# Larger score units and larger attention sums in a fused attention and two-layer kernel, under a new written order

## The chip, the cores and the metric

The kernel runs on one core of a Trainium2 chip. The metric is the device time of one execution in microseconds (us). Three runs of the kernel before gave 293.12, 293.34 and 293.79, median 293.34 us.

## The reference

Eight batches, eight heads, 576 positions, 64 values a head; q, k, v are fp32, drawn with a standard deviation of 0.1. Heads 0 to 3 see a window of 32 positions; heads 4 to 7 see every fourth position of the last 128. The rows of the attention, 4608 tokens x 512, go through two layers, 512 to 2048 and back to 512.

```python
scores = (q @ k.T) / 8
mask_plain = (rel >= 0) & (rel < 32)                     # heads 0-3
mask_dil = (rel >= 0) & (rel < 128) & (rel % 4 == 0)     # heads 4-7
attn = softmax(where(mask, scores, -1e9))
x = (attn @ v).transpose(0, 2, 1, 3).reshape(4608, 512)
h = x @ moe_w_in
out = (h * sigmoid(h)) @ moe_w_out                       # (4608, 512) fp32
```

## The kernel before

**The written order.** The whole kernel is a list of small steps, and TABLE (lines 11 to 121) is their order, written out by hand. Each word of it names a step, and every engine and every DMA queue works off its own instructions in that order. The first time a name stands there, a TensorE (PE) step issues its matmuls, and the letter behind "=" says in which PSUM bank (a, b, x, y, u, z; s is a pair of banks). Each later word of the same name issues the next instruction that follows: =A on ScalarE (ACT), =D on VectorE (DVE), =S a store on SP's queue, =P a sum on POOL; no letter, whatever engine the step has fixed. Steps without matmuls issue their first instruction at their first word. GpSimd (POOL) issues the casting loads and a few sums.

The names: the number in front is the batch, or, for l, y, u and t, the group of tokens. N0 to N3 cast raw q and k (0, 1 are k, 2, 3 are q), N4 to N11 clear the probability buffers; TD, TR, TA, TS transpose q and k on PE for batches 0 to 2 (PEB = 3); T are the transposing loads (SP's queue) that do this for batches 3 to 7; S is a score unit; V copies v, O shifts rows of v; P and D are attention sums of the plain and of the dilated heads; XP and XD transpose their outputs into xA, the input of layer 1; batches 5 to 7 write them to a scratch in DRAM (W, stores on SP) and read them transposed (X). L loads v for a batch and starts the cast of a later batch's q and k (its words: vraw, vp, cast); B does so for batch 2 and casts batch 3; M turns the additive mask into one of ones and zeros. l is layer 1, y layer 2, and u, w, v, a, t are the sums that the seven-product form of both layers needs (lines 885 to 943, 1004 to 1055). f are small POOL copies that hold loads back; z is a filler matmul (line 1082) into a bank nobody reads; exp and silu load an activation table ahead.

**Scores** (lines 601 to 647). A block is 128 keys by 96 queries (plain, "p", 12 a batch) or by 72 (dilated, "d", 16 a batch), for two heads (p) or two residues of a head (d) at once, each in a bank; the contraction is 64 long, so that a score matmul uses 64 of the 128 rows of PE's array. SETS says which blocks make a unit: batches 0 to 2 have seven units of four blocks, the others six (4, 4, 4, 6, 6, 4). A unit is one Exp, or one a bank, and one DVE multiply by its mask (line 647), read from mask_p or mask_d. Batch 0 (BIASED) has no multiply: the mask, as a large negative number, is put into the bank first by a matmul with the identity (line 616). Probabilities lie in 8 buffers (NP), taken in turn.

**Attention sums** (lines 685 to 712). The probabilities are the weights, v with a column of twos behind it the moving side: 65 columns, the last of which is the denominator. A block here is one head's 96 or 72 queries: 24 plain and 32 dilated a batch. A step takes four into one bank, then DVE does a reciprocal (line 691) and a multiply (line 693). A batch has 6 P steps (`av_p`) and 8 D steps (`av_d`). The dilated v goes from `vraws`, as loaded, to `vds` with its column of twos (line 671).

**Layers.** Groups of tokens are 256, 256, and then eight of 512. Group 0's layer 1 needs XP0 to XP2 and XD0 of batch 0. Groups 0 and 1 use plain layer 2 (line 954), the rest the seven-product form (line 1015); layer 1 uses line 830, and the seven-product form (line 918) for half of group 7 and for groups 8 and 9.

**The start.** Two loads on SP bring batch 0's raw k and q for the dilated heads; POOL issues the others. Lines 347 to 385 are memsets, the identity, the masks and the clears of the v buffers (lines 351 to 355, one ACT copy each); eight matmuls and the fillers keep PE running until data comes.

Of the kernel before, what the change touches and what calls it, by code (L numbers as in the profile page):

```python
# [19 lines left out]
l1.7=b 0B l1.2=s l1.7=t l1.7 l1.0=a l1.0=t l1.0 l1.15=y l1.15=s l0.13=u l0.14=x l1.3=y l0.14=s l1.3=t l0.15=a  # L20
l0.13=s l0.5=b l0.5=s l0.15=s 0B l0.9=u l1.3 0M l0.12=x l1.4=y 0N11=D l0.12=s l1.4=s l0.8=b l0.8=s l0.9=s
l1.6=z l1.1=x l1.1=s 1TD2=b l0.4=a l0.4=s 1TD2=D l1.6=s 1TD1=u 1TD1=D l1.10=y l1.10=s 1TA1k=a 1TA1k=A l1.12=z
1TD0=x l0.6=y l1.12=s l0.6=s 1TD0=D l1.11=a l1.11=s 1TD3=u 1TD3=D 1TA0k=y 1TA0k=D 1TA0q=x 1TA0q=D l1.9=z
1TS0=a 1TA1q=u 1S6=yb 1S6 1S6 l1.9=t 1TA1q=A 1V1=D 1O2 1TS1=x 1S3=s 1TS1=D y0.0.0=y 1TS1=D 1TS0=A 1TS0=A l1.9
1S3 l1.8=b w0 1S4=za 1S4 1S4 l1.8=t l1.8 l1.5=u 1S3 1S2=s 1S2 1S6 1S5=zx 1S5 y0.0.1 1S5 1S2 1S1=s l1.5=t l1.5
1S0=ba 1S0 1S3 y0.1.0=z l1.13=b 1S0 1V0=D l1.13=s 1D12=a y0.1.1 1D12 1S4 l1.14=x l1.14=s y0.1.2 1D01=u 1D12
# [100 lines left out]
def kernel(  # L127
# [12 lines left out]
    P = 128  # L140
# [983 lines left out]
```

## Time and profile before

| what | us |
|---|---|
| median of three runs (lowest, highest) | 293.34 (293.12, 293.79) |
| the profiled execution | 293.66 |
| its span, first instruction to last | 291.9 |
| its granted TensorE clock | 1.0 throughout |

The busy time of each engine by stage of that execution:

| stretch (us) | PE | DVE | ACT | POOL |
|---|---|---|---|---|
| 4.5 to 23.6 (batch 0 up to layer 1 alone) | 17.28 of 19.10 | 14.74 | 13.97 | 13.80 |
| 23.6 to 288.6 | 264.79 of 265.00 | 207.72 | 178.21 | 41.93 |
| 288.6 to 291.9 (last copies and stores) | 0.11 of 3.30 | 0.00 | 0.37 | 0.00 |

PE is the matmuls, PEld the weight loads, which overlap them. In the rows that follow L12 is line 12 of the kernel, "128x512 f16 x16" the shape of an operand and the number of instructions in a group; "[0.28 <-issue]" is idle time of the engine ahead of an instruction and what ended it.

### The profile page before, as it was taken

What the parts mean: (1) busy time and instruction counts of PE and PEld (TensorE: products, weight loads), DVE (VectorE), ACT (ScalarE), POOL (GpSimd) and SP (SyncE); (2) the same over time, 40 slices, a digit from 0 to 9 for tenths busy, and PEclk for the clock granted to TensorE, in tenths of its full rate; (3) what the DMA queues carried; (4) which work ended last, traced back from release to release, by engine and by line L of the source; (5) the groups of instructions that cost most, each with busy time, mean ns of one, the idle gap of its engine ahead of it and who ended that gap; (6) DMA issues with size and microseconds to landing.
All of it is one profiled execution on the core that took longest, in us unless ns stands there. A gap on an engine that the chain in (4) does not pass through costs nothing.

```text
span 291.9 us, 7564 instructions
## 1 busy us (share of the span) xinstructions
PE 285.5 (98%) x3006; PEld 205.1 (70%) x3006; DVE 225.3 (77%) x671; ACT 196.3 (67%) x411; POOL 58.8 (20%) x93
## 2 busy tenths in 40 slices
PE   7999999999999999999999999999999999999995
PEld 2568855655576777458567776588668888888884
DVE  5794477888985887666686869788999977949971
ACT  5787794598688477765966965548666656407931
POOL 8854724003720060034000071000000000000000
PEclk9999999999999999999999999999999999999999
DMA  8999999999999979989994749987620221112003
GB/s 158 183 202 197 192 195 186 201 186 187 128 206 202 209 126 199 184 160 82 216 200 78 196 74 192 237 190 186 182 61 24 78 57 74 54 56 110 3 2 142
DMA packets 98731, 42.30 MB, mean 145 GB/s; under 512 B 67208, under 2 KB 94344, under 8 KB 98696
## 3 DMA queue, kind: packets, MB, share of 16 engines
q0 software_dynamic: 46464, 19.21, 54.3%
q1 hardware_dynamic: 49784, 18.29, 29.2%
q10 hardware_dynamic: 2448, 4.33, 4.2%
q8 instruction: 23, 0.38, 0.5%
q14 instruction: 12, 0.10, 0.1%
HBM read 39.19 MB, written 17.10 MB: 193 GB/s over the span
## 4 chain that ended last, share of the span: by engine, by line
PE 90%; DMA 6%; POOL 2%; DVE 0%; issue 0%; ACT 0%; ACTq 0%
PE y L1015 33%; PE h L830 30%; PE h L918 11%; PE y L954 5%; DMA w_in<-in_moe_w_in_dram 4%; PE s L628 4%; PE av_d L688 3%; DMA nat<-in_q_dram 2%; PE av_p L688 2%; POOL w_in L388 1%; PE td L543 1%; PE xd L744 1%; PE xp L728 1%; POOL vp L333 1%; PE ta_k L577 0%; PE ta L590 0%
## 5 line engine op out<-in xcount | busy, mean ns | idle before, releaser
L830 PE MATMUL h<-xA,w_in 128*128 128x512 f16 (+1 forms) x480 | 101.5, 351 | 0.1
L839 ACT ACTIVATE gT<-h 128x512 f16<-128x512 f32 (+1 forms) x102 | 53.3, 543 | 29.2 <-PE h L830 28.1
L830 PEld LDWEIGHTS <-w_in 128*128 128x128 f16 x480 | 43.1, 97 | 30.7 <-DVE oD L693 0.5
L1015 PEld LDWEIGHTS <-gT 128*128 128x128 f16 x512 | 48.2, 98 | 6.9
L1015 PE MATMUL y<-w_out,gT 128*128 128x256 f16 x384 | 48.3, 273 | 0.0
L1015 PEld LDWEIGHTS <-work 128*128 128x128 f16 x384 | 36.7, 98 | 6.1 <-issue 0.3
L1015 PE MATMUL y<-w_sum,work 128*128 128x256 f16 x256 | 32.0, 273 | 0.1
L1042 DVE TENSOR_TENSOR ob<-y,nat 128x256 f32<-128x256 f32 x48 | 20.1, 421 | 14.2 <-PE y L1015 11.7
L688 PEld LDWEIGHTS <-probs 128*128 128x128 f16 x448 | 23.0, 97 | 10.6 <-ACT probs L637 0.6
L693 DVE TENSOR_TENSOR oD<-av_d,rcps 72x256 f16<-72x256 f32 x64 | 25.9, 414 | 1.1
L637 ACT ACTIVATE probs<-s 128x768 f16<-128x768 f32 (+2 forms) x29 | 22.5, 775 | 4.5 <-PE s L628 4.4
L642 ACT ACTIVATE probs<-s 128x384 f16<-128x384 f32 (+2 forms) x44 | 19.4, 492 | 3.6 <-PE s L628 3.1
L693 DVE TENSOR_TENSOR oP<-av_p,rcps 96x256 f16<-96x256 f32 x48 | 19.6, 414 | 0.7
L495 ACT COPY nat<-y 128x256 f32<-128x256 f32 x27 | 10.1, 375 | 13.1 <-PE y L1015 10.2
L691 DVE RECIPROCAL rcps<-av_d 72x4 f32<-72x4 f32 x64 | 10.0, 169 | 11.3 <-PE av_d L688 11.2
L1015 PE MATMUL y<-w_out,work 128*128 128x256 f16 x128 | 16.6, 273 | 0.0
L1015 PE MATMUL y<-w_sum,gT 128*128 128x256 f16 x128 | 16.6, 273 | 0.0
L495 ACT COPY vraw<-h 128x256 f32<-128x256 f32 x31 | 10.8, 380 | 8.5 <-PE h L918 8.5
L485 POOL COPY fence<-kqT 128x1 f16<-128x1 f16 x10 | 4.2, 442 | 59.2 <-DMA kqT<-kq_s 59.2
L688 PE MATMUL av_d<-vd,probs 128*128 128x65 f16 x256 | 15.7, 193 | 0.2 <-DVE vd L497 0.2
L954 PE MATMUL y<-w_out,gT 128*128 128x512 f16 x64 | 15.8, 379 | 0.0
L1077 POOL COPY fence<-gT 128x1 f16<-128x1 f16 x11 | 2.8, 282 | 63.9 <-ACT gT L839 32.5
(131 smaller groups left out, 503.8 us busy)
## 6 DMA issues: line engine op xcount, KB each, us to landing
out_dram<-ob SPq DMA_DIRECT2D x18, 256.0 KB, 2.1
out_dram<-ob ACTq DMA_DIRECT2D x16, 256.0 KB, 3.1
kq_s<-in_k_dram POOLq DMA_DIRECT2D x5, 576.0 KB, 9.2
kq_s<-in_q_dram POOLq DMA_DIRECT2D x5, 576.0 KB, 11.7
vp<-in_v_dram POOLq DMA_DIRECT2D x6, 384.0 KB, 7.7
w_out<-in_moe_w_out_dram POOLq DMA_DIRECT2D x4, 512.0 KB, 10.5
vraw<-in_v_dram POOLq DMA_DIRECT2D x10, 160.0 KB, 4.8
w_in<-in_moe_w_in_dram POOLq DMA_DIRECT2D x3, 512.0 KB, 8.9
```

The source lines that it names most:

```text
L495: nc.scalar.copy(dst, src)
L628: nc.tensor.matmul(sp[i][:, w * n : w * (n + 1)], lhs, rhs, start=not biased, stop=not biased or n == len(blocks) - 1,)
L637: nc.scalar.activation(p2, both[:, :, :n], AF.Exp, scale=scale)
L642: nc.scalar.activation(p2[:, i], sp[i][:, :n], AF.Exp, scale=scale)
L688: nc.tensor.matmul(a[:, i, : D + 1], lhs(i), rhs(i), start=True, stop=True)
L693: nc.vector.tensor_tensor(o, a[:n, :, :D], rcp[:n, :, None].broadcast_to([n, HN, D]), ALU.mult)
L830: nc.tensor.matmul(h[:, :w], w_in16[:, c, f * P : (f + 1) * P], x_g[:, c], start=(c == 0), stop=(c == HP - 1),)
L839: nc.scalar.activation(o, h[:, :w], AF.Silu, scale=2.0)
L918: nc.tensor.matmul(y, lhs[:, c, j], rhs[:, c], start=first and c == 0, stop=c == 1, skip_group_check=not first,)
L954: nc.tensor.matmul(y, gTs[g][:, f, tb * P : (tb + 1) * P], w_out16[:, f], start=(f == 0), stop=(f == NFF - 1),)
L1015: nc.tensor.matmul(y, lhs[:, c, tb * P : (tb + 1) * P], rhs[:, c], start=first and c == 0, stop=c == KP - 1, skip_group_check=not first,)
L1042: nc.vector.tensor_tensor(half, y, (u2, t5, t1)[n - 3], ALU.add)
```

## The change

Five things are edited, and the order is written anew.

- Score units: batch 0 keeps its seven units of four blocks; every other batch has five (5 p; 5 p; 2 p and 4 d; 7 d; 5 d). The two mask tiles become one, `mask`, of 7 x 96 and 9 x 72 columns, and STARTS says where a unit's mask begins in it. M becomes one instruction.
- Attention sums: a batch has four P steps of 6 blocks and five D steps of 6, 6, 7, 6 and 7 blocks, each with one reciprocal and one multiply.
- Batch 0's dilated v: its sums read `vraws` (64 columns) as loaded, and a matmul of one column, `twos`, gives each block's denominator. The V steps of batch 0 go; the row shift O2 of batch 0 writes `vraws`.
- Clears: seven probability buffers in place of eight, of 1008 + 128 columns. A memset of 64 columns behind the first use of each (EDGES, LEAD) stands at the start, and N4 to N10 clear what is left (304 or 496 columns, as two halves). The clears of `vraws` are four ACT copies in place of two.
- The order: TABLE is new throughout. Nine fillers stand in it in place of twelve. Among what moves: N2 (the first cast of q) stands ahead of N0; batch 3's second L word (vp) stands behind batch 4's second and third; layer 1 of group 0 begins behind the last of batch 0's sums.

The diff, with the table cut to lines that show this:

```diff
--- before.py
+++ after.py
-0N5=A z10 z22 0N1=D z1 z26 0N0=D z15 0N2=D 0TD0=x 0TD0=D 0TD1=a 0TD1=D 0N3=A 0TD3=u z24 0N4=A 0TA1k=z 0TD2=a
-0TD3=D 0TA1k=A 0TD2=A 0S3=s 0S3 0TA0k=x 0TA0k=D 0TA0q=a 0TA0q=D 0V0=D 0N7=D 0N8=A 0TA1q=z 0TA1q=A 0N6=D 0O0
-0N10=D 0S3 z12 0S4=s z14 0S4 0S4 0D00=u 0D00 0D00 0S1=bz 0S1 0D01=x 0S1 0D01 0D01 0S0=s 0TR=b 0D02=u 0D02 0D02
-0S0 0S0 0TS1=x 0TR=A 0TR=D 0D03=a 0D03 0D03 0P0=z 0P0 z23 0V1=A 0S6=s z13 0S6 0S6 0XD0=b 0O2 0P0 0XD0=A 0XD0=A
-0P2=u 0P2 0TS1=D 0TS1=A 0S5=s 0D13=z 0P2 z11 0D13 0D13 0O1 z9 0XP0=u 0P1=a 0P1 0P1 0N9=D 0S5 0S5 0TS0=z 0B
-0XP0=A 0TS0=A 0TS0=A 0P3=u 0XP2=b 0S2=s 0P3 0P3 0S2 0XP2=D 0XP1=y 0XP1=A 0D10=z 0D10 0D10 0S2 0D12=a 0D12 0D12
-0P5=x 0P4=z l0.0=u l0.0=s 0P5 0P5 l0.7=b 0P4 l0.7=s 0D11=x l0.2=a l0.2=s 0D11 0D11 l0.3=y 0P4 0XD1=b l0.3=s
-0XP4=a 0XD1=D 0XD1=A 0XP5=x 0XP5=D l0.1=z l0.1=s l0.10=u l0.10=s 0XP3=y 0XP4=D 0XP3=D l0.11=x l0.11=s l1.2=y
...
-l2.15=a 2P3 2P3 2XP3=z 2XD1=D 2XP3=A 2XP2=b y2.0.0=y u2.1=P 2XP2=D y0.1.3=A w1 2P5=b 3L 4L l3.0=x l2.15=s
...
-3S1 3S3 l3.6=z y2.0.6=D 3S5 l3.6=s l3.10=u l3.10=s 3D11=a 3D11 3S3 3S0 3L 2XP5=b 2XP5=D 4L l3.7=y l3.7=s
-y2.1.0=u 3D11 3P0=a 3P0 y1.1.3=S l3.13=y y2.1.0=A l3.4=s 3P0 3P1=z 3P3=b 3P1 l3.13=s l3.2=a y2.1.2 4L 3P1
...
-4XD1=z 6L 6L 6T y4.0.0=y 4XD1=D y3.1.6=A 5P5 4XP5=u 4XP5=A u4.0=D y4.0.1=a 4XD1=A y4.0.0=D l5.12=u y4.0.1=A
...
-y4.0.6 5S0 6T 5D10=z 5D10 5D03=u 5D03 y4.0.6=A y4.0.6=A 6T l5.7=a 5D03 l5.7=s 5D02=x 5D02 5D02 5W2 5P1=y 5P1
-5P1 y4.1.0=u 5P0=x 5P0 5D10 l5.3=b 5P0 5W0 6S2=s u5.2=D y4.0.5=A exp 6S2 l5.3=s 5D11=z 5D11 5D11 l5.1=y 6T
...
-y9.1.6=A y9.1.6=S
+0N2=D z2 0N0=D 0N1=A z4 0N3=A 0N7=A 0TD1=u 0TD0=x 0TD0=D 0TD2=b 0TD2=D z17 0TD3=x 0TD1=D z13 0TD3=D 0S3=az
+0TA0k=u 0S3 0S3 z20 0S4=s 0S4 0TA1q=b 0TA0k=D 0TA1q=D 0TA1k=u 0TA0q=x 0TA1k=D 0TA0q=A 0S1=xa 0S4 0D0=z 0D0
+0S0=s 0D0 0D1=b 0D1 0S1 0O2 0TS0=x 0S1 0TR=z 0S0 0O0 0D1 0S0 0P0=a 0TS0=A 0TS0=A 0TS1=u 0TR=D 0TR=D 0P1=x
+0S6=s 0N10=A 0N9=D 0S6 0S5=bz z1 0P0 0TS1=D 0P0 0TS1=D 0S5 0D2=u 0S5 0S6 0S2=s 0XP0=b 0P1 0P1 0D2 0D2 0XP2=z
+0XP1=a 0O1 z26 0XP0=A 0XP2=D 0D3=u 0XD0=z 0S2 0XD0=A 0XD0=A 0XP1=D 0D4=b 0S2 0P3=a 0B 0P2=x 0B 0D3 0D3 0D4 0D4
+z12 0P2 0P2 z29 l0.2=z l0.2=s 0P3 0P3 l0.0=u 0XP3=x l0.7=b l0.5=y l0.0=s l0.7=s 0XP3=D 0XP4=z 0XD1=u 0XP5=x
+0XP4=D 0XD1=A 0XD1=A l0.1=b 0N8=A l0.3=a 0XP5=D l1.2=x l0.1=s l0.5=t l1.2=s l1.6=u l1.6=s l0.5 0N4=A l0.3=t
...
+2D0 3L l2.5=s l2.15=s 2P2=z 2P0=x 2P0 2P2 2P0 l2.11=u l2.11=s 2P1=y 4L l2.9=x l2.9=s 2P1 2P2 2D4=b 2XD0=z
...
+2XP2=b 2XP2=D 2D3 2XD0=D y2.0.0=y 3S0=s u2.1=D 2XP0=x 2XP1=a 2P3=z 4L 2XD1=b 2XD1=A 2XD1=A y2.0.1=u u2.2=D
...
+3S1 y2.0.4 y2.0.3 y2.0.5 l3.15=x w0 3S3 3S3 3S2=za 3S4=s 3S4 y2.0.4 4L 3S2 3S2 y2.0.5 l3.7=b l3.7=t l3.7
...
+l3.6=b 2XP5=a 3L l3.4=s 2XP5=A l3.6=s 3V0=A 3P1=y 3P1 3P1 3P0=x l3.11=z l3.11=s 3P0 3P0 3XP2=b 3XP2=D 3P3=a
...
+4XD0=u 5S3=s 5S0=zx 5V0=A 4XP1=A 5S3 4XD0=D 4XD0=D 6L 5S0 y3.1.6=D 5S3 6L 5S0 u4.1=D u4.1=D l5.10=b 5S3 6T 5S1
+5S2=s 5S4=ya 5S0 6T l5.10=t 5S4 5S4 5S4 l5.10 5S2 5S2 l5.15=u l5.11=z l5.15=s l5.6=x 5S2 l5.6=s l5.5=a l5.9=b
...
+u4.2=D 5P3=a y3.1.5=A 4D3 y4.0.0=A 4D4 4D4 y4.0.1=b 6T y4.0.2 y4.0.2=A 4D3 4XP4=z y4.0.1=D y3.1.6=A 4XP4=D
...
+l5.12=u l5.12=s 4XP3=a 5D1 5W0 y4.1.0=b 4XP3=D 5W2 y4.1.0=A 5P2=a u5.2=D l5.1=s 5D3=u 6T 5D3 5D3 y4.1.1=x
+y4.1.1=A y4.1.2 5P2 y4.0.5=A 5P2 u5.0=P 5W3 5W1 6S0=uy 6S1=s 6S1 y4.1.2=D 6S0 6S0 y4.0.6=A 6S1 u5.1=P y4.1.3
+y4.1.3 y4.1.4 y4.1.5 y4.1.4 6S2=az 6S0 6S3=yu 6S4=s 6S2 6S3 5X0 6S2 y4.1.5 y4.1.5=S y4.1.6 y4.1.6=A y5.0.0=a
...
+y9.1.4 y9.1.6 y9.1.5 y9.1.5=A y9.1.6=A y9.1.6=A
...
     oD = cpool.tile([MH, 2, DIL, HN, D], F16, name="oD")
-    rcps = cpool.tile([P, NB + 2 * DIL, HN], F32, name="rcps")
+    rcps = cpool.tile([P, (NB + 2 * DIL) * HN], F32, name="rcps")
...
     LEAD = 64
+    EDGES = [2 * 4 * QB] * 3 + [2 * 4 * MH] * 4
     NW = HN * S
...
     }
+    twos = vds[1][:, 0, 0, 0, D : D + 1]
     as32 = [
...
     fence = cpool.tile([P, 2 + len(HOLD)], F16, name="fence")
-    mask_p = cpool.tile([P, 6, QB], F16, name="mask_p")
-    mask_d = cpool.tile([P, 10, MH], F16, name="mask_d")
+    MP, MD = 7, 9
+    mask = cpool.tile([P, MP * QB + MD * MH], F16, name="mask")
+    mask_p = mask[:, : MP * QB].rearrange("p (n c) -> p n c", c=QB)
+    mask_d = mask[:, MP * QB :].rearrange("p (n c) -> p n c", c=MH)
...
     for t in vraws:
-        nc.scalar.copy(
-            t.rearrange("p a h r d -> p (a h r d)").bitcast(F32).rearrange("p (n c) -> p n c", n=4),
-            warm.bitcast(F32)[:, None, :].broadcast_to([P, 4, GT // 2]),
-        )
+        for ab in range(2):
+            nc.scalar.copy(
+                t[:, ab].rearrange("p h r d -> p (h r d)").bitcast(F32).rearrange("p (n c) -> p n c", n=2),
+                warm.bitcast(F32)[:, None, :].broadcast_to([P, 2, GT // 2]),
+            )
     nc.gpsimd.affine_select(
...
     nc.vector.tensor_scalar(band, band, 1.0, BIG, ALU.subtract, ALU.mult)
-    nc.vector.tensor_copy(mask_d[:, :6], band[:, None, :MH].broadcast_to([P, 6, MH]))
-    nc.vector.tensor_copy(mask_d[:, 6:], band[:, None, MH - KB : 2 * MH - KB].broadcast_to([P, 4, MH]))
-    nc.vector.tensor_copy(mask_p, band[:, None, W:].broadcast_to([P, 6, QB]))
+    nc.vector.tensor_copy(mask_d[:, :4], band[:, None, :MH].broadcast_to([P, 4, MH]))
+    nc.vector.tensor_copy(mask_d[:, 4:], band[:, None, MH - KB : 2 * MH - KB].broadcast_to([P, MD - 4, MH]))
+    nc.vector.tensor_copy(mask_p, band[:, None, W:].broadcast_to([P, MP, QB]))
     nc.vector.memset(mask_p[:W, :2], -BIG)
...
     nc.vector.memset(kqDs[0][:, :, :, 0, MA:], 0.0)
+    for t, n in zip(probs, EDGES):
+        nc.vector.memset(t[:, n : n + LEAD], 0.0)
     for t in vps:
...
     POOLS = {"a": ps_h, "b": ps_h, "x": ps_x, "y": ps_y, "u": ps_y, "z": ps_z}
-    p_sets = [[("p", j, hp) for j in (2 * i, 2 * i + 1) for hp in range(HP // 2)] for i in range(3)]
+    p_all = [("p", j, hp) for j in range(NB) for hp in range(HP // 2)]
     d_all = [("d", ab, rp, h) for ab in range(2) for rp in range(2) for h in range(HN)]
     SETS = {
-        True: p_sets + [d_all[4 * i : 4 * i + 4] for i in range(4)],
-        False: p_sets + [d_all[:6], d_all[6:12], d_all[12:]],
+        True: [p_all[4 * i : 4 * i + 4] for i in range(3)] + [d_all[4 * i : 4 * i + 4] for i in range(4)],
+        False: [p_all[:5], p_all[5:10], p_all[10:] + d_all[:4], d_all[4:11], d_all[11:]],
     }
-    MASKS = {
-        True: [mask_p[:, 0:4], mask_p[:, 2:6], mask_p[:, 2:6], mask_d[:, 0:4], mask_d[:, 0:4],
-               mask_d[:, 6:10], mask_d[:, 6:10]],
-        False: [mask_p[:, 0:4], mask_p[:, 2:6], mask_p[:, 2:6], mask_d[:, 0:6], mask_d[:, 4:10],
-                mask_d[:, 6:10]],
+    STARTS = {
+        True: [0, 2 * QB, 2 * QB] + [MP * QB + n * MH for n in (0, 0, 4, 4)],
+        False: [0, 2 * QB, 5 * QB, MP * QB, MP * QB + 4 * MH],
     }
+    AV = {
+        "P": [(6 * n, 6 * n + 6) for n in range(4)],
+        "D": [(0, 6), (6, 12), (12, 19), (19, 25), (25, 32)],
+    }
+
+    def wide(blk):
+        return QB if blk[0] == "p" else MH
+
     HOME = {
-        p: {blk: (u, n) for u, blks in enumerate(sets) for n, blk in enumerate(blks)}
+        p: {
+            blk: (u, sum(map(wide, blks[:at])))
+            for u, blks in enumerate(sets)
+            for at, blk in enumerate(blks)
+        }
         for p, sets in SETS.items()
     }
+    SUMW = {p: [sum(map(wide, blks)) for blks in sets] for p, sets in SETS.items()}
...
         pe_path = b < PEB
-        sets, masks, home = SETS[pe_path], MASKS[pe_path], HOME[pe_path]
+        first = b in BIASED
+        sets, starts, home, widths = SETS[first], STARTS[first], HOME[first], SUMW[first]
         ns = len(sets)
-        base = sum(len(SETS[b_ < PEB]) for b_ in range(b))
+        base = sum(len(SETS[b_ in BIASED]) for b_ in range(b))
         vp, vd = vps[b % NV], vds[b % NV]
...
                 ]
-            blocks, mk = sets[u], masks[u]
-            w = mk.shape[2]
+            blocks, n = sets[u], widths[u]
+            mk = mask[:, starts[u] : starts[u] + n]
             biased = b in BIASED
             if biased:
-                bs = mk.rearrange("p a c -> p (a c)")
                 for i in range(2):
-                    nc.tensor.matmul(
-                        sp[i][:, : w * len(blocks)], ident, bs, start=True, stop=False
-                    )
-            for n, blk in enumerate(blocks):
+                    nc.tensor.matmul(sp[i][:, :n], ident, mk, start=True, stop=False)
+            for blk in blocks:
+                c = home[blk][1]
                 for i in range(2):
...
                     nc.tensor.matmul(
-                        sp[i][:, w * n : w * (n + 1)], lhs, rhs, start=not biased,
-                        stop=not biased or n == len(blocks) - 1,
+                        sp[i][:, c : c + wide(blk)], lhs, rhs, start=not biased,
+                        stop=not biased or blk == blocks[-1],
                     )
-            n = w * len(blocks)
             pt = probs_of[u] = probs[(base + u) % NP]
...
             yield
-            mk = mk.rearrange("p a c -> p (a c)")[:, None, :].broadcast_to([P, 2, n])
-            nc.vector.tensor_tensor(p2, p2, mk, ALU.mult)
+            nc.vector.tensor_tensor(p2, p2, mk[:, None, :].broadcast_to([P, 2, n]), ALU.mult)
...
             yield
-            c = 2 * 4 * MH
-            copy_on(eng, probs[n][:, c:], warm[:, : PW + P - c])
+            c = EDGES[n] + LEAD
+            w = (PW + P - c) // 2
+            copy_on(
+                eng, probs[n][:, c:].rearrange("p (a c) -> p a c", a=2),
+                warm[:, None, :w].broadcast_to([P, 2, w]),
+            )
...
             yield
-            for t in (mask_p, mask_d):
-                nc.vector.tensor_scalar(t, t, 1.0 / BIG, 1.0, ALU.mult, ALU.add)
+            nc.vector.tensor_scalar(mask, mask, 1.0 / BIG, 1.0, ALU.mult, ALU.add)
...
             yield
-            nc.vector.tensor_copy(vd[:KB, 1, :, :, :D], vraws[b % NV][KB : 2 * KB, 0])
+            dst = vraws[b % NV][:KB, 1] if b in BIASED else vd[:KB, 1, :, :, :D]
+            nc.vector.tensor_copy(dst, vraws[b % NV][KB : 2 * KB, 0])
...
         def prob_cols(blk, i):
-            u, n = home[blk]
-            c = (len(sets[u]) * i + n) * (QB if blk[0] == "p" else MH)
+            u, c = home[blk]
+            c += widths[u] * i
             return probs_of[u][:, c : c + P]
...
-        def av(ring, key, o, rcp, lhs, rhs):
-            a = small(ring, [P, HN, 66], F32, f"av_{b}_{key}")
-            for i in range(HN):
-                nc.tensor.matmul(a[:, i, : D + 1], lhs(i), rhs(i), start=True, stop=True)
-            n = o.shape[0]
-            yield
-            nc.vector.reciprocal(rcp[:n], a[:n, :, D : D + 1])
+        def av(ring, kind, n):
+            f0, f1 = AV[kind][n]
+            N = f1 - f0
+            a = small(ring, [P, N, 66], F32, f"av_{b}_{kind}{n}")
+            for f in range(f0, f1):
+                i = f % HN
+                if kind == "P":
+                    j = f // HN
+                    lhs, rhs = prob_cols(("p", j, i // 2), i % 2), vp[:, i * NB + j, : D + 1]
+                else:
+                    ab, r = f // HN // DIL, f // HN % DIL
+                    lhs, rhs = prob_cols(("d", ab, r // 2, i), r % 2), vd[:, ab, i, r, : D + 1]
+                    if b in BIASED:
+                        rhs = vraws[b % NV][:, ab, i, r]
+                        nc.tensor.matmul(a[:, f - f0, D : D + 1], lhs, twos, start=True, stop=True)
+                nc.tensor.matmul(a[:, f - f0, : rhs.shape[1]], lhs, rhs, start=True, stop=True)
+            at = 0 if kind == "P" else NB * HN
+            o = oP.rearrange("p j h d -> p (j h) d") if kind == "P" else oD.rearrange("p a r h d -> p (a r h) d")
+            m = o.shape[0]
+            rcp = rcps[:m, at + f0 : at + f1, None]
+            yield
+            nc.vector.reciprocal(rcp, a[:m, :, D : D + 1])
             yield
             nc.vector.tensor_tensor(
-                o, a[:n, :, :D], rcp[:n, :, None].broadcast_to([n, HN, D]), ALU.mult
-            )
-
...
+                o[:, f0:f1], a[:m, :, :D], rcp.broadcast_to([m, N, D]), ALU.mult
             )
...
             add(("O", 2), lambda eng: vd_shift(), False)
-        for j in range(NB):
-            add(("P", j), lambda ring, j=j: av_p(ring, j))
+        for n in range(len(AV["P"])):
+            add(("P", n), lambda ring, n=n: av(ring, "P", n))
         for ab in range(2):
-            add(("V", ab), lambda eng, ab=ab: vd_of(eng, ab), False)
-            for r in range(DIL):
-                add(("D", ab, r), lambda ring, ab=ab, r=r: av_d(ring, ab, r))
+            if b not in BIASED:
+                add(("V", ab), lambda eng, ab=ab: vd_of(eng, ab), False)
+        for n in range(len(AV["D"])):
+            add(("D", n), lambda ring, n=n: av(ring, "D", n))
```

More of the change, by code (lines that the diff above doesn't have):

```diff
@@ L22 @@
[L22 to L26, printed above, removed]
@@ L198 @@
     xA = cpool.tile([P, HP, GA * GT], F16, name="xA")
-    NP = 8
-    PW = 2 * 6 * MH
+    NP = 7
+    PW = 2 * 7 * MH
     probs = [cpool.tile([P, PW + P], F16, name=f"probs{i}") for i in range(NP)]
@@ L690, in av @@
             yield
-            nc.vector.reciprocal(rcp[:n], a[:n, :, D : D + 1])
+            nc.vector.reciprocal(rcp, a[:m, :, D : D + 1])
             yield
             nc.vector.tensor_tensor(
-                o, a[:n, :, :D], rcp[:n, :, None].broadcast_to([n, HN, D]), ALU.mult
-            )
-        def av_p(ring, j):
-            def lhs(i):
-                return prob_cols(("p", j, i // 2), i % 2)
-            yield from av(
-                ring, f"p{j}", oP[:, j], rcps[:, j], lhs, lambda i: vp[:, i * NB + j, : D + 1]
-            )
```

177 lines of the change are left out of this document (82 added, 95 removed).

## The prediction

> **What bounds the kernel now.** I read the page first (busy time, slices), then the chain of waits in order of time, the waits of PE, the timeline of the first 27 us, and the rows of DVE and ACT by form.
>
> ```profile
> span 291.9 us, 7564 instructions
> PE 285.5 (98%) x3006; PEld 205.1 (70%) x3006; DVE 225.3 (77%) x671; ACT 196.3 (67%) x411; POOL 58.8 (20%) x93
> ```
>
> PE is busy 98% and no other engine is over 77%. A busy PE can still lose time inside its records, so the chain says more (start, length, how many matmuls):
>
> ```profile
> 50.85 0.48 PE av_p L688 x16
> ...
> 82.97 0.63 PE s L628 x24
> 83.60 2.73 PE y L1015 x24
> ...
> 92.46 0.87 PE y L1015 x8
> ...
> 107.14 0.45 PE s L628 x16
> 107.59 0.98 PE y L1015 x8
> ...
> 119.07 3.45 PE h L830 x16
> ```
>
> From about 26 us the chain is PE all the way to 287.9, and each piece runs at a fixed pace: 0.87/8 = 0.109 us for a 256-column matmul, 3.45/16 = 0.216 for 512 columns, 0.48/16 = 0.030 for an attention matmul of 65. But y behind a score unit takes 0.98 where it takes 0.87 elsewhere, and 2.73 where 24 x 0.109 = 2.62. Scores show the same on the way in: 24 take 0.63, 16 take 0.45, so 0.0225 each and 0.09 over. Scores use 64 rows of the array, the rest all of it. **Each change between the two costs PE about 0.10 us**, with nobody to wait for; the waits call it issue:
>
> ```profile
> PEld L628 <- issue: 6.4, 24, 0.4
> ...
> PE av_p L688 <- ACT probs L637: 0.5, 1, 0.5
> ```
>
> Behind 26 us PE waits for another engine hardly at all: once each of 0.26 us (284.19) and 0.16 (274.42), and small ones; about 1 us in all. The first 26 us are different, a chain of latencies:
>
> ```profile
> 5.86 0.10 PEld L1083 LDWEIGHTS <-w_sum 128*128 128x128 f16 x1 [0.28 <-issue]
> 6.64 0.62 ACT L495 CAST nat<-kqT 96x512 f16<-96x512 f32 x1 [2.18 <-DMA kqT<-in_q_dram]
> 7.12 0.64 PE L552 MATMUL td<-ident_w,nat 96*128 96x96 f16 x11 [0.62 <-DVE nat L497]
> ...
> 19.84 0.43 PE L688 MATMUL av_p<-vp,probs 128*128 128x65 f16 x8 [0.47 <-ACT probs L637]
> ...
> 20.11 1.04 PE L830 MATMUL h<-xA,w_in 128*128 128x256 f16 x8
> ```
>
> q lands at 6.6, transposes run from 7.12, the last wait for probabilities ends at 19.84, layer 1 starts at 20.11 and is alone from 23.57. It then waits 0.27 us at 25.64 for the last part of w_in.
>
> **The change, part by part.** Durations are those of the profiled execution (293.66 us, span 291.9); the median of the runs is 293.34, so 0.3 is taken off at the end.
>
> *Score units*: 7 + 2 x 7 + 5 x 6 = 51 become 7 + 7 x 5 = 42. Matmuls and columns stay (448; 4608 columns a batch). What falls on PE is changes of array shape. I counted them in the two orders: take each PE step where it first appears, class it as score (64 rows), ta transpose (64 columns) or full, and count neighbours of different class (in batch 0 the mask matmul counts as full). Before 85, of them 21 in batch 0; after 67 and 20. In batches 1 to 7 that is 64 against 47: **17 x 0.10 = 1.7 us off PE in the stretch where PE is the bound.** The floor for one change is 0.09, the ceiling 0.12 (0.63 for 24 scores at 0.0215), so 1.5 to 2.0.
>
> *Exps and masks* (off the path): DVE multiplies of 576, 768 and 864 columns take 444, 544 and 595 ns, so 0.525 ns a column; widths of 960, 1008 and 720 give 645, 670 and 520. A batch pays 3.13 us in place of 3.41 or 3.27: 1.3 us of DVE in all. By the order ACT changes between Exp and Silu 18 times in place of 20, 2 x 1.28 us. The single mask multiply of 1296 + 24 columns costs what the two did (437 + 304 ns). PE covers all of it; uncovered it would be a gain.
>
> *Attention sums*: 14 pairs of reciprocal (169 ns) and multiply (414 ns at 256 columns) become 9. From 421 ns at 256 to 691 at 512 a PSUM column costs 1.05 ns, so multiplies of 384 and 448 take 548 and 616. Per batch 14 x 0.583 = 8.2 us become 9 x 0.17 + 7 x 0.548 + 2 x 0.616 = 6.6: 1.6 us off DVE, eight times. From 26 us on that is idle time off the path (DVE is 78% busy there). In batch 0, where DVE is busy 4.7 and 4.8 us of 5 between 10 and 20 us, it counts.
>
> *Batch 0's v*: one copy on DVE (0.60 us) and one on ACT (1.06) go; 32 one-column matmuls come. No row has one. They cost PE no less than nothing and, with the same weights loaded again, no more than the 65-column ones, 0.030: 0 to 0.96 us. I take 0.027, near that row since the load stays: 0.86.
>
> [...]
>
> *Clears*: eight of 416 columns (0.32 us DVE, 0.53 ACT) become seven, four of them moved behind layer 1's start; seven memsets of 64 columns (112 ns by the vds memset) are added ahead, 0.8 us at most, inside the 0.86 us that DVE waits before the cast at 4.90. The vraw clears become four copies; POOL waits for one less before the first v load (0.34 us now), and every later load of its queue may be issued that much earlier. The loads share bandwidth (200 GB/s), so I take nothing for it. Buffers fall from 8 to 7, but a batch takes 5 in place of 7 or 6: reuse is no nearer.
>
> *The start under the new order.* (a) DVE casts q (0N2) ahead of k (0N0); both are needed, and q is late, so the first transposes move from 7.12 to about 7.6: +0.45. (b) From there to layer 1, PE has 10.5 us of work before (rows times counts), and used 13.0: 2.5 of idle. After it has 10.5 + 0.86 - 0.1 (a change) + 0.1 (more of batch 0 stands ahead of layer 1) = 11.4, the seven filler matmuls there being seven again. (c) DVE has about 2.4 us less there; but the PE order puts whole tiles behind each other, the first score unit behind three transposes' copies and so on, so I take 0.5 of the idle away: 2.0 (bounds 1.0 and 3.5). That starts layer 1 at 7.6 + 11.4 + 2.0 = 21.0, or 0.8 later for equal work. (d) Steps 12 to 15, which waited 0.27 at 25.64, stand later in the new order, and layer 1 no longer runs between sums that wait (0.3). **Net +0.3 us, bounds -0.8 and +1.8.**
>
> *Loads moved.* Loads are issued in table order, but POOL and SP run ahead of PE. Batch 3's vp load moves behind batch 4's vp load and its two casts: POOL was through with those at 82.28; the casts landed at 90.22 and 93.08, and a vp load takes 5.9 to 8.0. So it lands between 88 and 101, say 96, where it landed at 84.10. 3P1 waits for it, and behind 3P1 all of PE. That step has 89.7 us of PE work ahead; PE ran 8 to 9 us behind its summed work before, so it is due near 98.5. I take no wait (0 to 2.5 us). The transposing loads of batches 5 and 6 stand earlier, except that 6T's last stays behind two x_s stores of batch 5 on SP: due near 167.5, landing about 167. Nothing again, up to 1 us.
>
> *Stalls* behind 26 us: 1 us before; the order is new throughout, with less on DVE and ACT. I keep 1 (0 to 2.5). The tail is the same pair of copies and stores, the last on ACT's queue in place of SP's (issue 0.34 and 0.33).
>
> **Sum:** -1.7 + 0.3 = -1.4. Span 290.5, that execution 292.3, **median 291.9 us.** Its own range: terms of +-1 us, 290.9 to 292.9.
>
> **The rivals.**
>
> *1. DVE and ACT were the hidden bound.* Against: 1 us of waits is all PE shows after 26 us. For: DVE is full from 10 to 20 us. Then the start gains its 0.8, half the stalls go: -1.7 - 0.8 - 0.5 = -3.0, 290.3 us.
>
> *2. Loads come late.* The vp load or 6T costs its upper bound, or PE meets a place in the new order that its rows do not show: about +1.5 on the sum, 293.4. The slack of 2.5 us speaks against, the load's place behind 1.15 MB of casts for it.
>
> *3. The 0.10 us does not go with the units.* If it hung on the matmuls (448 stay), the 1.7 would be 0 and the change not do what I count on: 293.6. The intercept 0.09 from 16 and 24 scores speaks against.
>
> *4. PE starts slow.* The filler matmuls start 0.427 us apart up to 5.86, then 0.216. PE has 13 of them ahead of the first transposes; after only 10, so it stops near 1.19 + 10 x 0.427 = 5.5, before that step, and idles 2.1 us to 7.6 (now 0.8). If the rise needs the same 4.7 us of matmuls, the transposes start at half pace: of the 4.1 us of work up to 12 us each costs double, some 1.5 in the idle: +2.5, the sum +1.1, **294.4 us**. It decides from the point where transposes stand 0.084 us apart in place of 0.042. Against it: the 0.8 us of idle did not lower the pace.
>
> [...]
>
> **How the numbers follow.** Forecast 0.54, rival 1 0.12, rival 2 0.14, rival 3 0.06, rival 4 0.14. A measurement of this kernel tells 0.2% (0.59 us) from no change. Faster, below 292.75: forecast and rival 1 but for 0.02, 0.64. Same: half of rivals 2 and 3 and the forecast's edge, 0.16. Slower: the other parts and rival 4, 0.20. The range runs from rival 1's 290.1 to rival 4's 294.4.
>
> **What would show it.** Right: "PEld L628 <- issue" falls, 42 exps' groups, av rows of 384 and 448 columns near 0.55 and 0.62, layer 1 alone from 23 to 24 us, no PE wait over 0.5 us after 26. Wrong: first transposes 0.084 apart (rival 4), a wait of 3P1 or 6S2 on a DMA (2), layer 1 before 19.5 (1), y behind scores still 0.98 as often as now (3).

## The result, and the profile after

The changed kernel took 296.67 us (median; 295.87 to 296.99) against 293.27 for the kernel before (293.12 to 293.79): ratio 1.0109, interval 1.0085 to 1.0133, or 3.4 us slower. The forecast was 291.9. Medians here are of all runs of a kernel; ratios leave out runs more than 1.5% above its fastest. The page of the profiled execution, in the lines that stand for those shown of before:

```profile
span 295.1 us, 7532 instructions
PE 285.8 (97%) x3035; PEld 206.7 (70%) x3035; DVE 213.9 (73%) x579; ACT 194.1 (66%) x402; POOL 62.7 (21%) x97
...
PEclk9799999979999999999999999999999999999999
```

The two sevens, in slices of 7.4 us, are the two losses of clock that follow. The trace is of the run of 296.82, with a mean granted clock of 0.987. The others read 0.987 (296.52) and 0.994 (295.87 and 296.99): all four lost clock, and what the untraced ones lost where is not known.

Most of what was meant to happen did. VectorE fell from 225.3 to 213.9 us busy. Changes of array shape on PE, counted record by record, fell from 85 to 67 (behind 26 us from 64 to 47), and cost 98 ns each before and 99 after beyond the time of the columns. The rows of the sums are as priced, 546 to 547 ns at 384 columns and 617 at 448:

```profile
L718 DVE TENSOR_TENSOR oD<-av_D,rcps 72x384 f16<-72x384 f32 x24 | 13.1, 547 | 0.4
L718 DVE TENSOR_TENSOR oD<-av_D,rcps 72x448 f16<-72x448 f32 x16 | 9.8, 617 | 0.3
```

What was lost lies in two places. The first 12 us on PE (start, length, idle before):

```profile
1.19 3.29 PE L342 MATMUL y_warm<-w_sum 128*128 128x512 f16 x8 [1.19 <-DVE w_sum L339]
4.32 0.59 PE L1092 MATMUL y_warm<-w_sum 128*128 128x512 f16 x2
7.21 0.95 PE L562 MATMUL td<-ident_w,nat 96*128 96x96 f16 x12 [2.29 <-DVE nat L506]
7.96 0.63 PE L1092 MATMUL y_warm<-w_sum 128*128 128x512 f16 x1
```

Fillers end at 4.9 and PE idles 2.29 us. The first six transposes still stand 0.042 us apart; from 7.47 on it is 0.080, and PE stays at half pace until 10.9. Busy times by stretch (each column an engine; the granted TensorE clock is the third from the end) show the same there and at a second place:

```profile
4.50:6.00 1.50, 0.42 (x2) 0.00 (x0) 0.00 (x0) 0.62 (x1) 1.50 (x3) 1.00 1.28 202
6.00:8.00 2.00, 0.79 (x13) 0.80 (x14) 1.06 (x3) 1.12 (x2) 1.46 (x3) 0.86 1.45 190
8.00:10.00 2.00, 2.00 (x18) 0.97 (x16) 1.18 (x4) 0.00 (x0) 1.87 (x4) 0.50 1.88 173
...
59.00:60.00 1.00, 0.56 (x19) 0.43 (x17) 0.96 (x4) 0.00 (x0) 0.00 (x0) 1.00 1.22 227
60.00:61.00 1.00, 0.24 (x12) 0.24 (x13) 0.06 (x1) 0.88 (x2) 0.00 (x0) 1.00 1.22 209
61.00:62.00 1.00, 1.00 (x44) 0.86 (x37) 0.68 (x2) 1.00 (x4) 0.00 (x0) 1.00 0.51 84
62.00:63.00 1.00, 1.00 (x9) 0.40 (x4) 0.88 (x3) 1.00 (x3) 0.00 (x0) 0.54 1.42 157
63.00:64.00 1.00, 1.00 (x7) 0.16 (x7) 0.00 (x0) 0.67 (x2) 0.00 (x0) 0.50 0.76 147
```

The chain of waits names the second:

```profile
52.51 1.74 PE y L963 x8
54.28 5.76 DMA out_dram<-ob
60.12 0.59 ACT ob L504
61.46 0.38 PE s L636 x14
62.12 1.82 PE h L839 x4
```

The timeline has the two waits that join them:

```profile
60.12 0.58 ACT L504 COPY ob<-y 128x512 f32<-128x512 f32 x1 [1.82 <-DMA out_dram<-ob]
...
60.76 0.36 PE L587 MATMUL ta_k<-ident_w,nat 96*64 96x96 f16 x8 [1.20 <-ACT ob L504]
```

A store of 256 KB, issued on ACT's queue at 54.28, lands at 60.04. Three output buffers go round; the copy of `y1.1.3` on ACT needs the one that this store holds, and ACT waits 1.82 us for it. PE's next step (2TA0k) needs the bank that this copy empties: PE waits 1.20 us. Then the clock is halved from 62.07 to 65.48, and four layer-1 matmuls take 1.82 in place of 0.86.

A sum over the whole span, worked out from the records with each PE step at the price of its rows (no view prints it): before, 278.1 us of work, after 276.6, so 1.5 saved. How far PE's real time stands behind this sum:

| at (us) | before | after |
|---|---|---|
| 26 | 9.1 | 10.5 |
| 58 | 7.8 | 8.8 |
| 66 | 7.9 | 12.0 |
| 270 | 9.0 | 13.3 |
| last matmul | 9.6 | 14.2 |

4.6 us lost, 1.5 saved: the 3.2 by which the spans differ, but for rounding. The columns differ by 1.4 at 26 us, 1.0 at 58, 4.1 at 66, 4.3 at 270 and 4.6 at the end: 3.1 come between 58 and 66. Of these 1.2 are the wait and 1.7 the 3.4 us at half clock behind it.

### The profile page after: what moved, and what is told of

It reads as the page before. It is cut to its first block, busy times and chain, and to the rows that moved or that the text cites. A ratio compares the mean times of both kernels' runs of the same rounds, so it can differ in the third digit from the quotient of the medians.

```text
span 295.1 us, 7532 instructions
## 1 busy us (share of the span) xinstructions
PE 285.8 (97%) x3035; PEld 206.7 (70%) x3035; DVE 213.9 (73%) x579; ACT 194.1 (66%) x402; POOL 62.7 (21%) x97
## 4 chain that ended last, share of the span: by engine, by line
PE 91%; DMA 4%; DVE 2%; ACT 1%; issue 0%; ACTq 0%; SPq 0%; DVEq 0%
PE y L1024 33%; PE h L839 31%; PE h L927 10%; PE y L963 4%; PE s L636 4%; PE av_D L710 3%; DMA out_dram<-ob 2%; PE av_P L710 2%; DMA kqT<-in_q_dram 2%; PE xp L736 1%; PE xd L752 1%; PE y_warm L1092 1%; PE s L625 1%; PE ta_k L587 0%; DVE nat L506 0%; DVE ob L1051 0%
## 5 line engine op out<-in xcount | busy, mean ns | idle before, releaser
L839 PE MATMUL h<-xA,w_in 128*128 128x512 f16 (+1 forms) x480 | 99.4, 353 | 0.0
L839 PEld LDWEIGHTS <-w_in 128*128 128x128 f16 x480 | 44.3, 98 | 34.0 <-issue 0.8
L504 ACT COPY nat<-y 128x256 f32<-128x256 f32 x34 | 12.6, 373 | 26.0 <-PE y L1024 15.3
L710 PEld LDWEIGHTS <-probs 128*128 128x128 f16 x448 | 20.8, 97 | 6.8 <-issue 0.5
L644 ACT ACTIVATE probs<-s 128x960 f16<-128x960 f32 (+4 forms) x23 | 20.7, 902 | 5.5 <-PE s L636 5.5
L649 ACT ACTIVATE probs<-s 128x480 f16<-128x480 f32 (+4 forms) x38 | 18.8, 549 | 7.0 <-PE s L636 6.9
L718 DVE TENSOR_TENSOR oD<-av_D,rcps 72x384 f16<-72x384 f32 (+1 forms) x40 | 22.8, 575 | 0.8
L653 DVE TENSOR_TENSOR probs<-probs,mask 128x960 f16<-128x960 f16 (+2 forms) x35 | 21.5, 632 | 0.4 <-ACT probs L649 0.3
L853 DVE SCALAR_TENSOR_TENSOR gT<-th,h 128x512 f16<-128x512 f32 (+1 forms) x20 | 11.6, 578 | 14.1 <-ACT th L851 14.1
L718 DVE TENSOR_TENSOR oP<-av_P,rcps 96x384 f16<-96x384 f32 x32 | 17.3, 546 | 0.6
L716 DVE RECIPROCAL rcps<-av_D 72x6 f32<-72x6 f32 (+1 forms) x40 | 7.4, 189 | 14.0 <-PE av_D L710 13.9
```

The lines of the kernel that those rows point to most:

```text
L504: nc.scalar.copy(dst, src)
L644: nc.scalar.activation(p2, both[:, :, :n], AF.Exp, scale=scale)
L649: nc.scalar.activation(p2[:, i], sp[i][:, :n], AF.Exp, scale=scale)
L653: nc.vector.tensor_tensor(p2, p2, mk[:, None, :].broadcast_to([P, 2, n]), ALU.mult)
L710: nc.tensor.matmul(a[:, f - f0, : rhs.shape[1]], lhs, rhs, start=True, stop=True)
L718: nc.vector.tensor_tensor(o[:, f0:f1], a[:m, :, :D], rcp.broadcast_to([m, N, D]), ALU.mult)
```

## The experiments

**Four kernels on the two losses.** `store_early` moves the store; `fill5` adds fillers; `both` does both; `before_less` takes fillers from the kernel before.

```diff
 store_early, both:
-1P1=b y0.0.3=A y0.0.3=A 1P2 y1.0.2 ... y1.0.3=A y1.1.2 1P0 1P0 1XP1=a y0.1.3=A w1
+1P1=b y0.0.3=A y0.0.3=A y0.1.3=A 1P2 y1.0.2 ... y1.0.3=A y1.1.2 1P0 1P0 1XP1=a w1
 fill5, both:
-0N1=A z4 0N3=A
+0N1=A z4 z90 z91 z92 z93 z94 0N3=A
 before_less:
-0N5=A z10 z22 0N1=D z1 z26 0N0=D z15 0N2=D
+0N5=A z10 0N1=D z1 0N0=D 0N2=D
```

> The changed kernel, with one store (y0.1.3's, on ACT's queue) moved ahead of the copy that it stood behind, so that it is issued about 2 us earlier. Theory A (the store holds an output buffer, the copy of y1.1.3 waits for it on ACT, PE waits for that copy 1.2 us, and the idle PE then loses half its clock for 3.4 us): no PE wait over 0.3 us near 60 us, granted clock 1.0 from 12 us to the end, and 1.4 + 1.7 = 3.1 us less: 293.6. Theory B (PE would wait there anyway, for the transposes' copies or for loads): the stall of about 1.4 us stays under another releaser, and the time is within 0.5 of 296.7.

Measured: 299.93 (296.55 to 300.78), ratio 1.0193 (1.0146 to 1.024). A miss, for a reason at the other end: in the profiled execution PE had not left half pace when its fillers ended, and transposes went from 0.080 us apart to 0.042 only at 23.95; the row "7.00 PE h L839 x64" of the chain (64 matmuls of layer 1, the x64 row below) starts at 28.75, in the changed kernel at 24.71. The granted clock reads 1.00 all that time, so this column alone doesn't show it. At 60 us PE's wait for the copy fell to 0.3, but a new wait of 1.1 came near 119, for VectorE's write into an output buffer. From the x64 row to the last matmul this execution takes 265.9 us, the changed kernel 267.1, so the stall's relief is there in part; the late start hides it, and behind the last matmul 4.4 us follow in place of 3.2. Two of the six runs took 296.6, the others 299.5 to 300.8; of the two no trace is kept. So neither theory held as put.

> The changed kernel, with five more filler matmuls ahead of the first transposes. Theory A (PE idles 2.3 us ahead of them and the granted clock then is 0.5 for 3.4 us): transposes stand 0.042 us apart in place of 0.080, the clock is 1.0 at 8 to 11 us, layer 1 starts about 1.1 us earlier, time about 295.6; the stall near 60 us stays. Theory B (the start is a chain of loads and copies, and PE's pace is hidden in it): layer 1 starts within 0.3 us of now, 296.6.

Measured: 296.72 (294.88 to 299.35), ratio 1.0093 (1.0068 to 1.0117). The median did not move, but the runs fall into two groups. Two took 294.88 and 295.23, at a mean granted clock of 0.998 and 1.0; four took 296.64 to 299.35, at 0.989 to 0.994. (One stretch of 3.4 us at half clock takes 0.006 off the mean.) The trace is of the run of 294.88. Its start came as Theory A has it: clock 1.0, and the x64 row at 23.51, 1.2 earlier. The store was issued earlier too, at 53.26, and landed at 59.14, 0.9 earlier; PE waited a little longer for the copy, and met a wait of 0.34 at 115 us that the later start had hidden. But this time no half clock followed the stall:

```profile
PE ta_k L587 <- ACT ob L504: 1.3, 1, 1.3
```

```profile
PEclk9999999999999999999999999999999999999999
```

**A later wait on a transfer takes back part of what is gained ahead of it**, here about 0.4 of 1.2. The rest of what the median lacks goes with the clock that four of the six runs lost; where in the run they lost it is not shown.

> The store moved and five fillers added. Theory A: both gains, 3.1 + 1.1 less: 292.5, which is 0.8 below the kernel before; the work saved on PE (1.5 us by its rows) then shows, less 0.3 to 0.7 of other waits. Theory B (the new order or the larger sums and units cost something in themselves that the clock only covers): 294 or more.

Measured: 294.81 (294.42 to 296.37), ratio 1.0047 (1.0034 to 1.006); the x64 row at 23.32. Both moves together gain 1.9 of the 4.2 that Theory A had. The trace is of the slowest of the five runs, 296.37, with a mean clock of 0.994; the other four read 1.0 and took 294.42 to 295.37, 1.65 less at their median, which is about the price of one stretch at half clock. In the trace that stretch stands behind the first stall, from 60.32 to 63.73. The store that was moved is issued at 51.15 and lands at 58.49, and PE still waits 1.0 us; the timeline shows a second place:

```profile
51.15 7.33 DMA out_dram<-ob
58.57 0.59 ACT ob L504
```

```profile
116.37 0.42 DVE L1051 TENSOR_TENSOR ob<-y,nat 128x256 f32<-128x256 f32 x1 [1.80 <-DMA out_dram<-ob]
116.71 0.42 DVE L506 COPY vd<-vraw 128x1024 f16<-128x1024 f16 x1
116.85 1.03 PE L1024 MATMUL y<-w_sum,gT 128*128 128x256 f16 x8 [1.24 <-DVE ob L1051]
```

> The kernel before, with three of its five fillers ahead of the first transposes taken out, so that ten matmuls stand there as in the changed kernel and PE idles some 1.7 to 2.4 us. Theory A (idle time alone takes the clock away): granted clock 0.5 for 3.4 us behind 7 us, in at least some of the runs, and 1 to 1.5 us more: 294.6. Theory B (something else in the changed start does it, the order of the casts or the extra memsets): 293.3 as before and a clock of 1.0.

Measured: 294.17 (293.08 to 295.43), ratio 1.0027 (1.001 to 1.0044), mean granted clocks of 0.988 to 1.0 over its runs, where the kernel before had 0.998 or more in those beside it. Theory A, in some of the runs: four of twelve took 293.08 to 293.42 at 0.999 or more, five took 293.86 to 294.92 at 0.993 or 0.994, so fewer fillers alone cost clock, and one stretch of it about 1.1 us. One run took 295.43 at 0.988. Two more took 295.1 and 295.4 at 1.0; a late first rise, as in `store_early`, would look so, but no trace of them is kept.

**Output buffers.** What both stalls share is the buffer. A fourth needs 2 KB more; the tanh tile in 16 bits makes the room (its values are rounded to 16 bits, all else is computed as before).

```diff
-            th = o32.tile([P, GT], F32, tag=f"th{turn('th', 2)}", name=f"th_{g}_{f}")
+            th = o32.tile([P, GT], F16, tag=f"th{turn('th', 2)}", name=f"th_{g}_{f}")
...
-            ob = obp.tile([P, DM], F32, tag=f"ob{turn('ob', 3)}", name=f"ob_{g}_{tb}")
+            ob = obp.tile([P, DM], F32, tag=f"ob{turn('ob', 4)}", name=f"ob_{g}_{tb}")
```

> The changed kernel with four output buffers in place of three (the tanh tile goes to 16 bits to make room), and nothing else. Theory C (the copies wait for an output buffer because stores of 256 KB take 6 to 8 us while batch 3's and 5's casts run; moving one store by 2 us could not help): no PE wait over 0.4 us near 60 and 117 us; 1.4 + 1.7 us less, 293.6 where the start keeps the clock that it had, with a spread of 2 us from the start alone. Theory B (PE would wait for the next thing): the stall stays in another form, 295.5 or more.

Measured: 293.51 (292.13 to 297.46), ratio 0.9982 (0.9956 to 1.0008). The profiled execution has the same start as the changed kernel's (half clock from 7.5 to 10.9, x64 row at 24.29), and no wait of PE behind 26 us over 0.3. So the two can be set side by side: from the x64 row to the last matmul 264.0 us in place of 267.1, 3.1 less, which is the stall and the clock behind it. The medians differ by 3.2. The wide spread is likely that of the start: the three slowest runs (296.67 to 297.46) read a clock of 1.0, which a late first rise would explain; they have no trace.

> Four output buffers and five more fillers. Theory A + C: start as in the kernel with fillers (layer 1's work 1 us ahead of the kernel before), no stall at 60 or 117, clock 1.0: the work saved shows, 292.1 (1.2 below the kernel before) and a spread under 1 us. Theory B: 293.5 or more.

Measured: 292.32 (291.83 to 292.44), ratio 0.9948 (0.9932 to 0.9964). The x64 row starts at 22.95. PE's waits in all, and the chain where the stall was:

```profile
PE y_warm L342 <- DVE w_sum L339: 1.2, 1, 1.2
PE s L625 <- ACT work L504: 0.6, 1, 0.6
PE av_P L710 <- DMA vp<-in_v_dram: 0.2, 1, 0.2
```

```profile
55.58 0.86 PE y L963 x4
56.89 0.37 PE xd L752 x8
58.94 0.97 PE h L839 x4
59.91 0.75 PE s L636 x32
```

PE goes through, and 1.1 us under the kernel before (with or without a fourth buffer, by `before_ob4`) is what the change is worth with its two losses mended.

> Control: the kernel before with four output buffers and the 16-bit tanh tile. No wait for an output buffer held PE there, so every theory expects 293.2 to 293.5.

Measured: 293.40, ratio 0.9997 (0.9984 to 1.0009). The buffer gives the kernel before nothing; it was free there.

**The price of a change of shape**, by doubling it:

```diff
+                if not biased and blk == blocks[len(blocks) // 2]:
+                    nc.tensor.matmul(
+                        sp[0][:, 511:512], ident, mask[:, :1], start=True, stop=True, skip_group_check=True
+                    )
```

> The kernel with fillers and four buffers, and in each of the 35 score units of batches 1 to 7 a matmul of one column over all 128 rows in the middle: two changes of array shape and one small matmul more a unit. If each change costs PE 0.095 us, 35 x (2 x 0.095 + 0.027) = 7.6 us more than without, 299.7. If the price went with units or matmuls and not with the change, 35 x 0.03 = 1 us, 293.1.

Measured: 299.76, ratio 1.0205 (1.0187 to 1.0224). It is 7.44 us above `fill_ob4`; for 35 units that is 0.213 each, and less the 0.027 of the small matmul, halved, 0.093 a change. The record count agrees: 137 changes in place of 67.

**VectorE's sums, and the one-column matmuls.**

```diff
 sums14:
+            h = N // 2 if kind == "P" or n == 0 else 0
+            parts = [z for z in (slice(0, h), slice(h, N)) if z.stop > z.start]
...
 twos2:
+                        nc.tensor.matmul(a[:, f - f0, D : D + 1], lhs, twos, start=True, stop=True)
```

> The kernel with fillers and four buffers, with the reciprocal and multiply of the four plain sums and the first dilated one of each batch done in two halves: 14 pairs a batch on VectorE again, as before the change, on the same matmuls. If VectorE's time there lies off the path (as the prediction has it, but for batch 0): within 0.5 us of 292.3. If VectorE was the hidden bound: about 8 x 1.6 us of work come back, and a good part of it shows: 295 or more.

Measured: 293.53, ratio 1.0007 (0.9998 to 1.0016): 1.2 more than without. Neither "off the path" nor the bound. From the x64 row (23.57) to the end of the span it takes 268.2 us, without the edit 267.1: the 1.1 lies behind the start, in steps of 0.1 to 0.3 on PE (at 55.12, 215.61 and 270.94 on VectorE, by the trace). The edit gives back less than it was meant to: halves issued back to back overlap (64 of 0.345 us fill 19.4 us), and VectorE's busy time went from 213.3 to 217.5 us, 4.2 more, where the change had taken off 11.4. So 4 us of VectorE's work cost about 1 us of time here, and what the larger sums are worth in all is not bounded by this run.

> The kernel with fillers and four buffers, with each one-column matmul of batch 0's denominators issued twice: 32 more of them, 0.87 us of PE by the 0.027 that they stand apart in the trace of the changed kernel. If PE's work bounds the start (the prediction charged it in full): 293.2. If they lie in PE's waits for copies and probabilities there: 292.3 to 292.6.

Measured: 292.80, ratio 0.9987 (0.9978 to 0.9995): 0.5 of the 0.87 shows in the medians. (The x64 rows of one execution each differ by 0.97, 23.92 against 22.95, but with the same fillers that row also came at 23.32 and 23.51 without the edit.) The charge of the prediction was right by about half.

**Why the stores are slow.** Batch 3's casts run at the same time, 46 to 63.5 us. Both kernels here have the store and the fillers of `both`, and hold the casts (their word 0B moves behind y1.0.3's copy, and 3T's first word behind that):

```diff
 late_cast:
+        nc.gpsimd.tensor_copy(fence[:QB, :1], oP[:, 0, 0, :1])
         issue_cast(PEB)
 late_cast2:
+        nc.gpsimd.tensor_copy(fence[:QB, :1], oP[:, 4, 2, :1])
         issue_cast(PEB)
```

> The kernel with fillers and the store moved (three output buffers), with batch 3's casts of q and k held on POOL's queue until batch 1's plain sums of three steps are written, so that they start near 52.5 us in place of 46. Theory C1 (the stores of 256 KB took 5.8 to 7.7 us because the casts shared the DMA engines): the two stores issued near 50.7 land within about 3.5 us, the copy of y1.1.3 does not wait for them, and PE does not stop near 59 us. Theory C2 (stores on ACT's queue are that slow by themselves): they land after 5 us or more again and the stall stays. By both, batch 3's transposing loads then end near 79 us, where its first score unit is due, so a new wait of 0 to 3 us may stand there, and the time alone decides nothing.

Measured: 294.86, ratio 1.0048 (1.0036 to 1.0061). The hold did not hold: the casts were issued at 47.98, the store took 7.13, the stall stayed (0.7). It tells nothing of the two theories.

> As the run before, whose hold read rows of the plain output that were ready early, so that the casts still started at 48.0; here the hold reads a row of the last of the three sums, written at about 52.4 us, and the casts start behind that. Theory C1 (the casts slow the stores): the stores of 50.7 land within about 3.5 us and PE does not stop near 59 us. Theory C2 (the stores are that slow by themselves): they land after 5 us or more and the stall of about 1 us stays. A new wait of 0 to 3 us for batch 3's transposing loads near 79 us may come by both; the time alone decides nothing.

Measured: 293.59 (292.1 to 294.74), ratio 1.0011 (0.9989 to 1.0032). POOL and ACT:

```profile
52.26 0.58 POOL L438 COPY fence<-oP 96x1 f16<-96x1 f16 x1 [7.05 <-DVE oP L719]
52.78 0.79 POOL L283 DMA_DIRECT2D kq_s<-in_k_dram  x1
```

```profile
56.90 0.59 ACT L505 COPY ob<-y 128x512 f32<-128x512 f32 x1 [0.17 <-DMA out_dram<-ob]
```

The stall near 59 is gone, but the stores still took about 6 us (50.49 to 56.28 and 50.90 to 56.9), not 3.5: holding the casts back gained 1.1 to 1.3 us on the 7.1 and 7.3 before. The casts still began at 52.8, beside the last 4 us of the stores, and batch 2's vp load ran until 57 too, so this run lessens the overlap and does not end it; what the rest of the time is stays open. ACT's queue alone it is not: over the whole span of the changed kernel its 16 stores of this size take 2.6 us at the median, and in the kernel before one on SP's queue, issued at 47.65 among the same loads, took 5.66. The wait at 113.5, for a buffer, stayed (0.9).

## Why the prediction was wrong

- **Score units: right.** -1.7 was taken for 17 changes; 17 fewer were counted behind 26 us, at 0.093 by `tick` and 0.099 by the records.
- **Attention sums: the price nearly right, the cover in part wrong.** Reciprocals of 6 and 7 blocks took 0.18 to 0.19 in place of 0.17, so 1.4 us came off a batch, not 1.6. "Idle time off the path" does not hide VectorE's work wholly: PE's waits of about 1 us before were read as no dependence on it, and 4.2 us more busy time there bring back about 1 us (`sums14`).
- **Batch 0's v: right.** The one-column matmuls stand 0.027 apart in the changed kernel's trace, as taken.
- **First transposes at 7.6: wrong by 0.4.** They came at 7.21; the order of the casts cost 0.1 at most.
- **The start: rival 4's loss came, by another road.** It was given 0.14. PE did idle (from 4.9 to 7.2) and transposes did stand 0.080 apart, but rival 4 has the clock not yet risen. In the changed kernel's trace it had risen at 4.04, with the fillers still running, and it fell again at 7.46 behind the idle time: the first six transposes ran at full pace. Not yet risen is what `store_early` shows, until 23.95. The prediction argued the rival away with an idle time of 0.8 us that had cost nothing; 0.8 and 2.3 are not the same case. Its price of 2.5 was too high for this road, where the half clock ends after 3.4 us and some of it lies in waits: the medians of `ob4` and `fill_ob4` make it 1.2, the runs of `before_less` 1.1.
- **The step that failed is the term *Stalls* ("I keep 1").** No term looked at what a y step needs besides PE: an output buffer, and so a store that has landed. The order of the stores was read only for SP's loads (6T behind two x_s stores), not for the copies that wait on them. By the table, losses behind 26 us were 3.7 in place of the 0.5 before, and 3.1 of them stand at this one place: 1.2 of wait, 1.7 for 3.4 us at half clock, 0.2 not assigned. Rival 2 does name "a place in the new order that its rows do not show", at about +1.5; that fits the wait and leaves out that a stalled PE can also lose its clock (0.5 from 62.07 to 65.48 here).
- **Moved loads: right.** No PE wait on batch 3's vp load or on batch 6's transposing loads stands in the trace. The load landed at 98.86 and 3P1 ran from 101.86; without the stall, in `fill_ob4`, it was 93.02 and 97.14.

The range ended at 294.4. Stall and clock together, twice, were outside it because each was priced as if the other could not follow from it. Two small slips in the prediction's numbers change none of this: rival 1's own time is 290.3, not the 290.1 that the range begins with, and its chances for same and slower add up to 0.12 and 0.24 by their parts, not 0.16 and 0.20.

## What to carry to other kernels

Where PE is busy throughout, price a stall as the wait plus the half clock that may follow it (1.2 and 1.7 us here; it followed in the changed kernel and in `both`, not in the trace of `fill5`), and ask of each step which buffer its copy writes and when that buffer's last store lands. Before crediting a gain in an early stage in full, look for the next wait on a transfer: here the store landed 0.9 earlier where PE came 1.2 earlier. A median that does not move can hide two groups of runs, so set run times beside the mean clock of each. In this reordered kernel spare depth (one buffer, a few fillers) came ahead of further savings: it turned 3.4 us lost into 1.1 won.

## What the runs showed of the hardware that was not expected

In the changed kernel the granted clock fell at 7.46 and 62.07 and rose at 10.87 and 65.48. Its trace has five stretches between two changes, from 4.04 to 294.18 us, and each is a whole multiple of 3.41 us: 1, 1, 15, 1 and 67 times. The one stretch that the kernel before has, 286.72 us, is 84 times that. What sets the length is not shown.

Nor does idle time alone decide when the clock falls. Some of PE's waits of about 1 us and more, and the clock behind them:

| run | PE's wait, and where it ends (us) | idle (us) | clock behind it |
|---|---|---|---|
| changed kernel | for VectorE's cast, 7.21 | 2.29 | halved, 7.46 to 10.87 |
| `ob4` | the same, 6.94 | 2.0 | halved, 7.5 to 10.9 |
| changed kernel | for ACT's copy, 60.76 | 1.20 | halved, 62.07 to 65.48 |
| `both` | the same | 1.0 | halved, 60.32 to 63.73 |
| `fill5` | the same | 1.3 | kept |
| `both` | for VectorE's sum, 116.85 | 1.24 | kept |
| `late_cast2` | for VectorE's cast | 1.0 | kept |

What else decides stays open; no run separates it.

When PE first reaches full pace differs too: at 4.04 in the changed kernel, at 5.86 in the kernel before, and at 23.95 in `store_early`, where PE was busy for all of the 9.20 us from 14.80 to 24.00. That the spread of the kernels with ten filler and warm-up matmuls ahead of the first transposes comes from this is the author's estimate; the one trace of a late rise is that of `store_early`.

In these traces the granted clock as printed reads 1.0 up to its first change, also where matmuls still run at half pace (1.00 in `store_early` up to 24 us, with transposes 0.080 apart). So the "1.0 throughout" given for the kernel before holds only from 5.86 us on: its fillers stand 0.427 us apart up to there, and 0.216 after.
